# The last 64 tokens' values and gates in fp32, their products in column halves; the first keys on ScalarE's queue, the last rows stored in two parts, and a new order

## The chip, the cores and the metric

The kernel runs on one core of one Trainium2 chip. The metric is the device time of one execution in microseconds, lower is better. A core has a matrix engine (TensorE; PE in the profile, its weight loads PEld), VectorE (DVE), ScalarE (ACT), GpSimd (POOL) and SyncE (SP), which here issues the DMAs. Each engine works through its own instructions in the order in which the program lists them and waits where a semaphore has not been reached. Matmuls write into PSUM, 8 banks of 512 fp32 columns; DVE and ACT empty them.

## What is computed

Two parts, one feeding the other, for 8 batches of 576 tokens.

```python
# part 1: linear attention, 8 heads of 64, 128 features
proj = x @ w_phi                          # x is q or k
proj = proj - max(abs(proj), axis=-1)
phi  = concat([exp(proj), exp(-proj)])
kv   = phi(k).T @ v ;  z = sum(phi(k))
x    = (phi(q) @ kv) / (phi(q) @ z + 1e-6)    # 576 tokens x 512 (all heads side by side)
...
# part 2: 4 experts of head size 64, causal softmax attention, best 2 of 4 by gate
logits = x @ w_gate
for e in range(4):
    q, k, v = x @ wq[e], x @ wk[e], x @ wv[e]
    a  = softmax(causal(q @ k.T / 8))
    ye = a @ v @ wo[e]
    out += (e among the best two) * weight[e] * ye
```

## The kernel before, in words

The work is cut into 32 pairs of heads (four pairs make a batch) for part 1 and 8 batches of two expert groups (g = 0 and 1) for part 2. Each is a set of Python generators that yield one step after the other; a step belongs to one engine. The table `PICKS` holds two letters for each step: which generator goes next, and which PSUM bank it takes or whether ACT or DVE does a copy. So the whole order of every engine is a string that was written ahead, and `in_order` pins it. No rule in the program decides anything at run time; engines only wait for each other's semaphores.

Part 1, for a pair: `load_k`, `load_q`, `load_v` issue loads on SP two pairs ahead; `stream_k` and `stream_tail` project keys (L355, and L403 for the last 64 tokens); `center` (L389, L391) subtracts the row maximum on DVE; ACT takes two exponentials; `stream_kv` forms kv (L403); `stream_q`, `phi_q` project queries (L355), reduce over partitions on POOL (L494) and exponentiate; `stream_n` multiplies (L403); `normed` divides on DVE; `turn_x` transposes on DVE, writes to DRAM (`xd`) and reads it back as x with features on partitions, tile `xl`. x is then split into `xh` (fp32r) and `xl` (the rest), so that a product of full accuracy is three fp32r products: high by high, high by low, low by high.

Part 2, for a batch (`stream_b`): `proj_t` projects q and k of a group (L180), `proj_v` projects values and gate logits of all experts at once: for each of five token blocks j (four of 128 tokens, the last of 64) 12 products of 260 columns, 4 chunks of 128 features by the three fp32r combinations. `evac_v` copies a block from PSUM to `vl`. `scores` forms q @ k.T (L622), `soft` masks and copies, `post` takes the maximum (POOL, L494), subtracts (DVE, L740), exponentiates (ACT) and multiplies with the values (L403), `norm_y` divides and applies the gate weight, `turn_y` transposes (L446), `project_out` multiplies with `wo` (L180), `evac_o` copies to `ot`, `store` writes 128 rows of the output. `gates` works out the gate weights on DVE from the logits in `vl`. In batches 0 to 6 the order of parts is p0 v0 s0 p1 s1 (projections, values, scores); in the last batch it is p0 s0 p1 s1 v0.

The PSUM writes of L180 use the whole array (128 rows by 128 columns); L355 and L622 use it as two halves of 64 rows, L403 as two halves of 64 columns. An fp32 product of the program shows in the trace as two matmul instructions, an fp32r one as one.

At the start `keep_warm` puts 96 small bf16 products (L180, tile `warm`) on PE between the first projections. `split_piece` splits the weights into high and low parts; the values' and gates' weights (`vg`) come in two pieces of 520 columns.

The lines of the values' loop that the change is about:

```python
            for j in range(NJ):
                m = min(128, S - 128 * j)
                kc, ps = yield Step('PE', [k for c in xk for k in c], 'c', has('av', b - 1, 1) if b else has('w', 2))
                ...
                        mm(ps[:m, 0:260], xs[c][x_][:, 128 * j:128 * j + m],
```

## Time and profile before

| | |
|---|---|
| time, median of 3 runs | 567.36 us (566.82 to 567.86) |
| the profiled execution | 567.63 us, of which the span of its records is 565.8 us |
| TensorE clock granted | full in all 40 slices of the span |
| PE busy | 98% of the span |
| DVE, ACT, POOL busy | 86%, 70%, 34% |
| DMA | 62.37 MB, 40.9% of 16 engines' span |

All sums below are made against the profiled execution, which is 0.27 us above the median. A busy share is an average over the whole span; the views by stretch and the chain of waits tell which engine is waited for at a place.

### The profile page before, as it was taken

What the parts mean: (1) busy time and instruction counts of PE and PEld (TensorE: products, weight loads), DVE (VectorE), ACT (ScalarE), POOL (GpSimd) and SP (SyncE); (2) the same over time, 40 slices, a digit from 0 to 9 for tenths busy, and PEclk for the clock granted to TensorE, in tenths of its full rate; (3) what the DMA queues carried; (4) which work ended last, traced back from release to release, by engine and by line L of the source; (5) the groups of instructions that cost most, each with busy time, mean ns of one, the idle gap of its engine ahead of it and who ended that gap; (6) DMA issues with size and microseconds to landing.
All of it is one profiled execution on the core that took longest, in us unless ns stands there. A gap on an engine that the chain in (4) does not pass through costs nothing.

```text
span 565.8 us, 22762 instructions
## 1 busy us (share of the span) xinstructions
PE 555.6 (98%) x9744; PEld 524.6 (93%) x9744; DVE 486.3 (86%) x1246; ACT 395.7 (70%) x748; POOL 193.3 (34%) x78
## 2 busy tenths in 40 slices
PE   8999999999999999999999999999999999999997
PEld 7888899999999999999999999899999999999996
DVE  6899889889799988998998899899688897895893
ACT  4888888857748676686776596496676776665662
POOL 3735552323120752235503222522252430302320
PEclk9999999999999999999999999999999999999999
DMA  6978564533634653243534426334541121321013
GB/s 162 238 194 198 155 161 95 124 91 103 135 100 113 155 131 93 85 134 90 125 99 105 137 56 150 89 106 133 131 123 54 47 61 36 98 83 46 2 44 127
DMA packets 83317, 62.37 MB, mean 110 GB/s; under 512 B 47248, under 2 KB 66064, under 8 KB 83216
## 3 DMA queue, kind: packets, MB, share of 16 engines
q1 hardware_dynamic: 83216, 60.92, 40.9%
q8 instruction: 77, 1.26, 1.0%
q14 instruction: 24, 0.20, 0.1%
HBM read 42.02 MB, written 18.87 MB: 108 GB/s over the span
## 4 chain that ended last, share of the span: by engine, by line
PE 92%; DVE 3%; ACT 2%; issue 1%; ACTq 0%; DVEq 0%
PE ps_c L180 38%; PE ps_c L403 35%; PE ps_c L355 11%; PE ps_c L622 8%; PE ps_c L446 1%; ACT u L189 1%; DVE top L654 0%; DVE st L740 0%; ACT ek L191 0%; DVE gw L723 0%; DVE gs L721 0%; DVE xl L185 0%; DVE u L504 0%; DVE yl L185 0%; ACT mx L191 0%
## 5 line engine op out<-in xcount | busy, mean ns | idle before, releaser
L494 POOL PARTITION_ALL_REDUCE mx<-u x32 | 126.2, 3962 | 157.7 <-ACT u L189 106.8
L180 PE MATMUL ps_c<-xh,qk 128*128 128x320 f32 (+1 forms) x512 | 107.1, 300 | 0.5 <-DVE yl L185 0.5
L191 ACT ACTIVATE ek<-ek 128x1152 f32<-128x1152 f32 x64 | 74.8, 1169 | 20.2 <-DVE ek L391 19.3
L180 PEld LDWEIGHTS ps_c<-xh,qk 128*128 128x128 f32 x512 | 83.3, 189 | 2.3 <-DVE yl L185 0.7
L403 PE MATMUL ps_c<-v_in,ek 128*64 128x65 f32 x2560 | 81.6, 222 | 0.7 <-ACT u L189 0.7
L403 PEld LDWEIGHTS ps_c<-v_in,ek 128*64 128x64 f32 x2560 | 78.0, 137 | 3.9 <-ACT u L189 0.8
L189 ACT COPY st<-ps_c 128x288 f32<-128x288 f32 (+1 forms) x120 | 52.4, 503 | 34.1 <-DVE ps_c L642 29.4
L494 POOL PARTITION_ALL_REDUCE tops<-top x15 | 54.2, 3617 | 63.2 <-DVE top L654 63.2
L180 PE MATMUL ps_c<-xl,qk 128*128 128x256 f32 (+1 forms) x256 | 75.7, 296 | 0.0
L403 PE MATMUL ps_c<-kv,mx 128*64 128x65 f32 x1152 | 62.3, 223 | 1.8 <-ACT kv L189 1.4
L389 DVE TENSOR_REDUCE pmax<-ps_c 128x4 f32<-128x512 f32 (+1 forms) x96 | 51.3, 548 | 13.6 <-PE ps_c L355 7.5
L403 PE MATMUL ps_c<-kv,u 128*64 128x65 f32 x1152 | 59.9, 221 | 0.7 <-issue 0.7
L180 PE MATMUL ps_c<-vg,xh 128*128 128x260 f32 (+1 forms) x320 | 59.0, 285 | 0.0
L740 DVE TENSOR_TENSOR st<-st,tops 128x1152 f32<-128x1152 f32 (+4 forms) x75 | 57.4, 818 | 0.1
L189 ACT COPY u<-ps_c 128x256 f32<-128x256 f32 (+3 forms) x131 | 44.1, 423 | 15.7 <-PE ps_c L355 15.0
L391 DVE TENSOR_TENSOR ek<-ps_c,pmax 128x512 f32<-128x512 f32 (+1 forms) x96 | 52.0, 554 | 3.5 <-PE ps_c L403 1.1
L191 ACT ACTIVATE st<-st 128x1152 f32<-128x1152 f32 (+3 forms) x60 | 49.0, 866 | 8.4 <-DVE st L740 8.0
L403 PEld LDWEIGHTS ps_c<-kv,mx 128*64 128x64 f32 x1152 | 48.4, 138 | 5.1 <-ACT kv L189 2.3
L180 PE MATMUL ps_c<-yh,wo 128*128 128x256 f32 (+1 forms) x256 | 52.1, 298 | 0.0
L403 PEld LDWEIGHTS ps_c<-kv,u 128*64 128x64 f32 x1152 | 48.1, 138 | 0.9 <-issue 0.9
L180 PEld LDWEIGHTS ps_c<-xl,qk 128*128 128x128 f32 x256 | 48.5, 190 | 0.0
L403 PE MATMUL ps_c<-vl,st 128*64 128x65 f32 x1500 | 47.6, 222 | 0.7 <-issue 0.4
(110 smaller groups left out, 1187.2 us busy)
## 6 DMA issues: line engine op xcount, KB each, us to landing
v_in<-in_v_dram SPq DMA_DIRECT2D x32, 320.0 KB, 4.2
q_in<-in_qt_dram SPq DMA_DIRECT2D x64, 144.0 KB, 3.4
xl<-xd SPq DMA_DIRECT2D x32, 288.0 KB, 3.1
out_dram<-ot SPq DMA_DIRECT2D x32, 288.0 KB, 2.1
k_in<-in_kt_dram SPq DMA_DIRECT2D x32, 160.0 KB, 3.7
xd<-xt SPq DMA_DIRECT2D x64, 80.0 KB, 2.0
k_in<-in_kt_dram SPq DMA_DIRECT2D x32, 128.0 KB, 3.6
xd<-xt SPq DMA_DIRECT2D x64, 64.0 KB, 1.8
```

Of the source, the lines that this page charges most:

```text
L180: nc.tensor.matmul(o, a, b, start=start, stop=stop, skip_group_check=True)
L189: nc.scalar.copy(o, i)
L191: nc.scalar.activation(o, i, func, **kw)
L355: nc.tensor.matmul(o, a, b, start=True, stop=True, skip_group_check=True)
L389: dve(n * 128, [mk], [pk]).tensor_reduce(out=m[:, us], in_=src, axis=AX.X, op=ALU.max, apply_absolute_value=True)
L391: dve(n * 128, [(f'ek{p % EKB}1', us.start)], [pk, mk]).tensor_tensor(out=ek2[p % EKB][:, 1, us, :], in0=src, in1=m[:, us].unsqueeze(2).to ...
L403: nc.tensor.matmul(o, a, b, start=start, stop=stop, skip_group_check=True)
L446: nc.tensor.transpose(ps[:, 128 * n:128 * n + k], o[0:k, i, :], ident[0:k, 0:k])
L494: nc.gpsimd.partition_all_reduce(o, i, 128, op)
L622: nc.tensor.matmul(pp_[e][:, o:o + q1 - q0], kk2[k_][r, 128 * j:128 * j + 128], q2[q_][r, q0:q1], start=m == 0, stop=m == 2, skip_group_ch ...
L740: dve(2 * n, [sj[j]], [*key, mk], port=True).tensor_tensor(out=a, in0=a, in1=tops[x][0:m, :, 128 * j:], op=ALU.subtract)
```

## The change

1. The last block of `proj_v` (64 tokens, 12 products of 260 columns) goes. A new generator `tail_v` takes its place: for each of the 4 feature chunks two fp32 products of 130 columns, one into PSUM partitions 0 to 63 (experts 0 and 1 with their logits), one into partitions 64 to 127 (experts 2 and 3), as halves of 64 columns of the array (`column_mm`). It is spawned at the first part of a batch, so that its step can stand anywhere from there. Two copies of 130 columns (ACT or DVE) take the place of one of 260.
2. It needs x and the weights unsplit. The weights are copied by POOL into a new tile `wvf` (`whole_w`, 6 copies at the start). x's last 64 tokens come by an additional DMA for each pair from `xd` into `xf` (32 KB, 128 rows of 256 bytes), issued by SP behind the read of `xl`.
3. The first pair's three key loads are issued by ACT instead of SP.
4. The last 128 output rows are stored in two parts, columns 0 to 255 as soon as they are copied, then 256 to 575.
5. `col`, `row` and `warm` lie in tiles that are used later (`ot`, `ge`); this frees room for the new tiles.
6. `PICKS` is a new string: the order of all engines, the banks, and the choice of ACT or DVE for the copies. Counted over the order of each engine, ACT gets all 6 of DVE's copies to `kv` and all 10 of DVE's copies to `ot`, 12 of the 16 new copies to `vl`, and both casts of `vg`; DVE gets 2 casts of `yh` and 1 of `qk`. The number of warm products stays 96, and so does every other count of PE's instructions.

```diff
--- before.py
+++ after.py
@@ -50,51 +50,51 @@
 
 CODE = "ABCDEFGHIJKLMNOPQRSTUVWXYZabcdefghijklmnopqrstuvwxyz0123456789-_"
 PICKS = (
-    "BAAADADABABABABAAAAAAAAAAAAAAAAAAAGROANAGjNANACAG1OAOAG6PAOAEZPIQIQIPIDAFEBAPIPICANANIDAEAEAAAAAAAE1QIPIPIPIIAHAAAAAAAAA"
...
+    "BAAADACACADAEAAAAAAAAAAAAAAAAAAAHROAOAHjOAOAF1PIQIQIPIAAAAAAH5QAPAHaPAPADADAGECAEAQIQIOAOIJAFAFAF-RIQIQIQIOAOAIAGBPICAPI"
...
 )
 
 
@@ -206,12 +206,14 @@
 
     copies_sb = copies
 
-    def load(o, i, w, r=(), rate=90.0):
-        nc.sync.dma_start(o, i)
-
-    warm = sb("warm", [128, 128], BF16)
+    def load(o, i, w, r=(), rate=90.0, eng='SP'):
+        (nc.scalar if eng == 'ACT' else nc.sync).dma_start(o, i)
+
+    ot = [sb(f"ot{i}", [128, S]) for i in range(2)]
+    ge = sb("ge", [128, 5, 4, 4])
+    warm = ge.rearrange("p a b c -> p (a b c)").bitcast(BF16)[:, 0:128]
     nc.vector.memset(warm, 1.0)
-    col, row = sb("col", [128, 128]), sb("row", [128, 32])
+    col, row = ot[0][:, 0:128], ot[1][:, 0:32]
     nc.vector.memset(col[:, 0:1], 0.0)
     for k in range(7):
         n = 2 ** k
@@ -266,11 +268,11 @@
     nc.vector.memset(vl[:, :, :, 65:66], 1.0)
     nc.vector.memset(vl[64:128, NJ - 1], 0.0)
     lg = vl[:, :, :, 0]
-    ge = sb("ge", [128, 5, 4, 4])
     gt, gs = sb("gt", [128, 3, 5, 4]), sb("gs", [128, 2, 5])
     gw = sb("gw", [128, 5, 4])
     ys = [[sb(f"y{p}{g}", [128, S], F32R) for p in "hl"] for g in range(2)]
-    ot = [sb(f"ot{i}", [128, S]) for i in range(2)]
+    wvf = sb("wvf", [128, WVG])
+    xf = [sb(f"xf{i}", [128, 64]) for i in range(PXB)]
 
     wsp = {}
 
@@ -286,7 +288,7 @@
     def split_piece(name, c0, c1, st, src):
         hi, lo = wsp[name][0:2]
         key, m = st.tensor.name, c1 - c0
-        yield Step('SP', pred=has('w', 1 if name == 'wo' else 0))
+        yield Step('SP', pred=has('wvf', c0 - 520) if name == 'vg' and c0 else has('w', 1 if name == 'wo' else 0))
         load(st[:, 0:m], src[:, c0:c1], key, rate=50.0)
         st_ = Step(copies_sb(m), [key], port=True)
         yield st_
@@ -298,6 +300,7 @@
         else:
             h_, l_ = (t[:, c0:c1].rearrange("p (c n d) -> p c n d", n=4, d=65) for t in (hi, lo))
             x = st[:, 0:m].rearrange("p (c x) -> p c x", x=260)
+            plan.spawn(whole_w(key, x, c0, c1))
             for c in range(2):
                 copy(st_.eng, 256, h_[:, c, :, 1:65], x[:, c, 0:256].rearrange("p (n d) -> p n d", d=64), [hk], [key], 0.52)
             copy(st_.eng, 8, h_[:, :, :, 0], x[:, :, 256:260], [hk], [key], 0.52)
@@ -306,6 +309,14 @@
                 sub_lo(256, l_[:, c, :, 1:65], x[:, c, 0:256].rearrange("p (n d) -> p n d", d=64), h_[:, c, :, 1:65], lk, [key, hk])
             sub_lo(8, l_[:, :, :, 0], x[:, :, 256:260], h_[:, :, :, 0], lk, [key, hk])
 
+    def whole_w(key, x, c0, c1):
+        yield Step('POOL', [key])
+        f_ = wvf[:, c0:c1].rearrange("p (c n d) -> p c n d", n=4, d=65)
+        for c in range(2):
+            nc.gpsimd.tensor_copy(f_[:, c, :, 1:65], x[:, c, 0:256].rearrange("p (n d) -> p n d", d=64))
+        nc.gpsimd.tensor_copy(f_[:, :, :, 0], x[:, :, 256:260])
+        done.add(('wvf', c0))
+
     def load_phi():
         yield Step('SP')
         load(wf, wts[:, 0:WP], 'wphi')
@@ -337,11 +348,11 @@
 
     def load_k():
         for p in range(NPAIRS):
-            yield Step('SP', pred=(lambda: ('main_k', p - IB) in done and ('tail_k', p - IB) in done) if p >= IB else None)
+            yield Step('SP' if p else 'ACT', pred=(lambda: ('main_k', p - IB) in done and ('tail_k', p - IB) in done) if p >= IB else None)
             x, key = k_in[p % IB], f'k_in{p % IB}'
-            load(x[0:64, :], kt[p][:, 0:KC], (key, 0), rate=60.0)
-            load(x[64:128, 0:512], kt[p][:, 768:1280], (key, 1), rate=60.0)
-            load(x[64:128, 512:KC], kt[p][:, 640:768], (key, 2), rate=60.0)
+            load(x[0:64, :], kt[p][:, 0:KC], (key, 0), rate=60.0, eng='SP' if p else 'ACT')
+            load(x[64:128, 0:512], kt[p][:, 768:1280], (key, 1), rate=60.0, eng='SP' if p else 'ACT')
+            load(x[64:128, 512:KC], kt[p][:, 640:768], (key, 2), rate=60.0, eng='SP' if p else 'ACT')
             done.add(('load_k', p))
 
     def load_q():
@@ -541,8 +552,9 @@
         for a, (t0, t1) in enumerate(XROWS):
             load(hbm[:, :, t0:t1], xt[k][32 * a:32 * a + 32, :, 0:t1 - t0], (f'xd{k}', a), [b])
         done.add(('xw', p))
-        yield Step('SP', [(f'xd{k}', a) for a in range(4)], pred=(lambda: p < PXB or ('px', (p - PXB) // NP) in done))
+        yield Step('SP', [(f'xd{k}', a) for a in range(4)], pred=(lambda: p < PXB or all((x, (p - PXB) // NP) in done for x in ('px', 'pt'))))
         load(lo.bitcast(F32), xd[k], [f'xr{i}', f'xl{i}'], [(f'xd{k}', a) for a in range(4)])
+        load(xf[i], xd[k][:, 512:S], f'xf{i}', [(f'xd{k}', a) for a in range(4)], rate=32.0)
         done.add(('xd', p))
         xr = [f'xr{i}']
         st_ = Step(copies_sb(S), xr, port=True)
@@ -660,8 +672,8 @@
 
         def proj_v():
             wvg = wsp["vg"]
-            for j in range(NJ):
-                m = min(128, S - 128 * j)
+            for j in range(4):
+                m = 128
                 kc, ps = yield Step('PE', [k for c in xk for k in c], 'c', has('av', b - 1, 1) if b else has('w', 2))
                 n = 0
                 for c in range(4):
@@ -672,9 +684,26 @@
                         n += 1
                 plan.spawn(evac_v(j, m, kc, ps))
 
+        def tail_v():
+            xk_ = [f'xf{(b * NP + c) % PXB}' for c in range(NP)] + [('vg', 2, c0) for c0 in (0, 520)]
+            kc, ps = yield Step('PE', xk_, 'c', has('av', b - 1, 1) if b else (lambda: ('wvf', 0) in done and ('wvf', 520) in done), tiling=(128, 64))
+            for c in range(NP):
+                for e in range(2):
+                    o = 260 * c + 130 * e
+                    column_mm(ps[64 * e:64 * e + 64, 0:130], xf[(b * NP + c) % PXB], wvf[:, o:o + 130], c == 0, c == 3, kc, [xk_[c], xk_[4 + c // 2]], 130)
+            done.add(('pt', b))
+            for e in range(2):
+                st = Step(copies(130), [kc], hot=True)
+                yield st
+                copy(st.eng, 130, vl[0:64, 4, 2 * e:2 * e + 2, 0:65], ps[64 * e:64 * e + 64, 0:130].rearrange("p (n d) -> p n d", d=65), ['vs4'], [kc])
+            plan.release('c', (kc, ps))
+            done.add(('v', b, 4))
+
         yield Step('PE', (), None, lambda: all_x(*range(b * NP, b * NP + NP))() and all(('w', i) in done for i in (0, 1, 4)))
         for part in ORDER[b == B - 1]:
             yield Step('PE')
+            if part == ORDER[b == B - 1][0]:
+                plan.spawn(tail_v())
             g = int(part[-1])
             if part[0] == 'p':
                 yield from proj_t(0, g)
@@ -820,8 +849,15 @@
 
     def store(b, t):
         oks = [('ot', t % 2, p_[0]) for p_ in PARTS]
-        yield Step('SP', oks, pred=lambda: all(('ot', b, t, p_[0]) in done for p_ in PARTS))
-        load(out[b, 128 * t:128 * t + 128, :], ot[t % 2], ('out', b, t), oks)
+        last = b == B - 1 and t == 3
+        yield Step('SP', oks[:1] if last else oks, pred=(lambda: ('ot', b, t, 0) in done) if last else lambda: all(('ot', b, t, p_[0]) in done for p_ in PARTS))
+        if b < B - 1 or t < 3:
+            load(out[b, 128 * t:128 * t + 128, :], ot[t % 2], ('out', b, t), oks)
+        else:
+            for n, (s0, s1) in enumerate(PARTS):
+                if n:
+                    yield Step('SP', [oks[n]], pred=has('ot', b, t, s0))
+                load(out[b, 128 * t:128 * t + 128, s0:s1], ot[t % 2][:, s0:s1], ('out', b, t, n), [oks[n]])
         done.add(('out', 4 * b + t))
 
     for gen in (load_phi(), keep_warm(), zeros(), load_k(), load_q(), load_v(), stream_k(), stream_tail(), stream_q(), weights(w_qk, ('w', 1)), weights(w_vg, ('w', 2)), weights(w_wo, ('w', 3)), stream_kv(), stream_n(), stream_s()):
```

How the rows move, at three places.

TensorE, batch 0, the end of the values before the change, followed by the first scores (`vg` weights, `xh` and `xl` chunks, numbers are buffers):

```order
L180 MATMUL ps_c3_64<-vg_185,xl3_153 128x260
L180 MATMUL ps_c1_62<-vg_185,xh0_146 64x260 x2
L180 MATMUL ps_c1_62<-vg_185,xl0_147 64x260
L180 MATMUL ps_c1_62<-vg_185,xh1_148 64x260 x2
L180 MATMUL ps_c1_62<-vg_185,xl1_149 64x260
L180 MATMUL ps_c1_62<-vg_185,xh2_150 64x260 x2
L180 MATMUL ps_c1_62<-vg_185,xl2_151 64x260
L180 MATMUL ps_c1_62<-vg_185,xh3_152 64x260 x2
L180 MATMUL ps_c1_62<-vg_185,xl3_153 64x260
L622 MATMUL ps_c5_66<-qh_167,kkh_169 128x288
```

and TensorE, batch 0, with the change, ahead of the first projection of the batch (the key rows are a later pair's):

```order
L366 MATMUL ps_c4_65<-wf_121,k_in0_107 128x128
L414 MATMUL ps_c5_66<-wvf_181,xf0_182 64x130 x2
L414 MATMUL ps_c5_66<-wvf_181,xf1_183 64x130 x2
L414 MATMUL ps_c5_66<-wvf_181,xf2_184 64x130 x2
L414 MATMUL ps_c5_66<-wvf_181,xf3_185 64x130 x2
L414 MATMUL ps_c2_63<-wf_121,k_in0_107 64x128 x2
L180 MATMUL ps_c7_68<-xh0_146,qk_188 128x256
```

The 12 products behind the values are gone, and 8 narrower ones stand ahead of the batch's first projection, next to a key tail that uses the array in the same halves.

VectorE, last batch, around the first scores (L642 masks them; L415 to L440 divide the result of batch 6, group 1), before:

```order
L586 SCALAR_TENSOR_TENSOR ql_168<-ps_c6_67,qh_167 128x320
L642 TENSOR_TENSOR ps_c3_64<-ps_c3_64,mask_95 128x128
L642 TENSOR_TENSOR ps_c2_63<-ps_c2_63,mask_95 128x128
L415 TENSOR_SCALAR sc1_164<-ps_c0_61 128x5
L415 TENSOR_SCALAR sc1_164<-ps_c5_66 128x5
L420 RECIPROCAL ps_c5_66<-sc1_164 128x10
L421 TENSOR_TENSOR sc1_164<-ps_c5_66,gw_177 128x10
L434 TENSOR_TENSOR yq1_166<-ps_c0_61,sc1_164 128x4x64
L440 TENSOR_SCALAR yq1_166<-ps_c0_61,sc1_164 64x64
L434 TENSOR_TENSOR yq1_166<-ps_c5_66,sc1_164 128x4x64
L642 TENSOR_TENSOR ps_c1_62<-ps_c1_62,mask_95 128x128
```

and with the change:

```order
L185 TENSOR_TENSOR kkl_170<-ps_c4_65,kkh_169 128x320
L426 TENSOR_SCALAR sc1_164<-ps_c0_61 128x5
L426 TENSOR_SCALAR sc1_164<-ps_c7_68 128x5
L431 RECIPROCAL ps_c7_68<-sc1_164 128x10
L432 TENSOR_TENSOR sc1_164<-ps_c7_68,gw_176 128x10
L445 TENSOR_TENSOR yq1_166<-ps_c0_61,sc1_164 128x4x64
L451 TENSOR_SCALAR yq1_166<-ps_c0_61,sc1_164 64x64
L445 TENSOR_TENSOR yq1_166<-ps_c7_68,sc1_164 128x4x64
L654 TENSOR_TENSOR ps_c5_66<-ps_c5_66,mask_95 128x128
L654 TENSOR_TENSOR ps_c6_67<-ps_c6_67,mask_95 128x128
```

The seven dividing instructions now stand ahead of the first two masks instead of behind them.

SyncE, the first loads of the program, before:

```order
L210 DMA wf_121<-in_wts_dram 128x128
L210 DMA q_in0_109<-in_qt_dram 64x576 x2
L210 DMA q_in1_110<-in_qt_dram 64x576 x2
L210 DMA k_in0_107<-in_kt_dram 64x640
L210 DMA k_in0_107<-in_kt_dram 64x512
L210 DMA k_in0_107<-in_kt_dram 64x128
L210 DMA k_in1_108<-in_kt_dram 64x640
```

and ScalarE's first rows with the change (SyncE's list there goes on from `q_in0` straight to `k_in1`, then `q_in1`):

```order
L210 DMA k_in0_107<-in_kt_dram 64x640
L210 DMA k_in0_107<-in_kt_dram 64x512
L210 DMA k_in0_107<-in_kt_dram 64x128
L189 ACT_TABLE_LOAD
L189 COPY u0_126<-ps_c1_62 128x2x5x32
```

The first keys no longer stand behind four query loads, and ScalarE issues three loads ahead of its table load.

## Rows read from the trace of the kernel before

**Rows 1.** The page: busy time of PE (part 1), and the chain of work that ended last by engine (part 4).

```profile
PE 555.6 (98%) x9744; PEld 524.6 (93%) x9744; DVE 486.3 (86%) x1246; ACT 395.7 (70%) x748; POOL 193.3 (34%) x78
...
PE 92%; DVE 3%; ACT 2%; issue 1%; ACTq 0%; DVEq 0%
```

**Rows 2.** Busy time by stretch: stretch in us, its length, busy us of PE, PEld, DVE, ACT and POOL with counts, granted PE clock, DMA share, GB/s.

```profile
0.00:20.00 20.00, 18.00 (x256) 15.47 (x258) 14.73 (x62) 11.84 (x20) 9.78 (x9) 1.00 0.73 194
20.00:70.00 50.00, 48.24 (x1174) 42.47 (x1170) 43.85 (x99) 42.70 (x74) 25.85 (x7) 1.00 0.75 189
...
190.00:250.00 60.00, 60.00 (x1003) 56.87 (x1003) 55.23 (x126) 46.12 (x83) 24.52 (x9) 1.00 0.43 113
```

**Rows 3.** Who PE waited for: waiter, releaser, us in total, times, longest. The first and the last of seven rows; the seven add up to 6.1 us.

```profile
PE ps_c L403 <- issue: 1.5, 3, 0.7
...
PE ps_c L403 <- ACT st L191: 0.2, 1, 0.2
```

**Rows 4.** Timeline of PE, batch 0, the last value block (128*64 is the stationary tile) and the first scores: start, duration from first start to last end, instruction, count.

```profile
82.92 0.40 PE L180 MATMUL ps_c<-vg,xh 128*64 128x260 f32 x2
...
84.23 0.28 PE L180 MATMUL ps_c<-vg,xl 128*64 128x260 f32 x1
84.44 0.40 PE L622 MATMUL ps_c<-qh,kkh 64*128 64x288 f32 x2
```

**Rows 5.** Timeline of PE, three places with fp32 products in column halves (tile 128*64), each with the row that follows it.

```profile
62.08 0.44 PE L403 MATMUL ps_c<-wf,k_in 128*64 128x128 f32 x4
62.35 2.50 PE L403 MATMUL ps_c<-v_in,ek 128*64 128x65 f32 x80
64.78 1.24 PE L355 MATMUL ps_c<-q_in,wf 64*128 64x320 f32 x8
...
70.26 0.44 PE L403 MATMUL ps_c<-wf,k_in 128*64 128x128 f32 x4
70.63 0.39 PE L180 MATMUL ps_c<-xh,qk 128*128 128x256 f32 x1
...
546.39 3.14 PE L403 MATMUL ps_c<-vl,st 128*64 128x65 f32 x100
549.35 3.15 PE L403 MATMUL ps_c<-vl,u 128*64 128x65 f32 x100
```

**Rows 6.** Groups of instructions by form: line, engine, operation, tiles, shapes, count, busy us, mean ns of one, idle before. Copies that are moved or resized, on ACT, DVE and POOL.

```profile
L189 ACT COPY ot<-ps_c 128x320 f32<-128x320 f32 x28 | 12.2, 436 | 7.8 <-PE ps_c L180 6.2 <-DMA out_dram<-ot 1.6
L189 ACT COPY kv<-ps_c 128x260 f32<-128x260 f32 x26 | 9.8, 375 | 5.2 <-PE ps_c L403 5.0
L189 ACT COPY ot<-ps_c 128x256 f32<-128x256 f32 x26 | 9.7, 376 | 7.1 <-DMA out_dram<-ot 6.1 <-DVE top L654 0.9
L189 ACT COPY vl<-ps_c 64x260 f32<-64x260 f32 x5 | 1.8, 369 | 2.2 <-PE ps_c L180 2.0
...
L202 DVE COPY kv<-ps_c 128x260 f32<-128x260 f32 x6 | 2.5, 416 | 0.0
...
L635 POOL COPY top<-st 128x256 f32<-128x256 f32 x15 | 6.1, 405 | 115.8 <-ACT st L189 97.9 <-ACT gt L191 14.2 <-DVE sc L421 3.6
```

**Rows 7.** Timelines of the last batch: PE's product with the values of batch 6, DVE's masks and division behind it, the two reductions on POOL, DVE's last subtractions and ACT's last exponential.

```profile
517.17 3.22 PE L403 MATMUL ps_c<-vl,st 128*64 128x65 f32 x100
...
521.02 0.50 DVE L642 TENSOR_TENSOR ps_c<-ps_c,mask 128x128 f32<-128x128 f32 x2 [0.54 <-PE ps_c L622]
521.43 0.22 DVE L415 TENSOR_SCALAR sc<-ps_c 128x5 f32<-128x5 f32 x2
...
523.01 1.00 DVE L642 TENSOR_TENSOR ps_c<-ps_c,mask 128x128 f32<-128x128 f32 x4
...
528.81 3.58 POOL L494 PARTITION_ALL_REDUCE tops<-top  x1 [5.55 <-DVE top L654]
...
541.95 3.58 POOL L494 PARTITION_ALL_REDUCE mx<-mx  x1 [7.91 <-DVE mx L654]
...
545.57 3.76 DVE L740 TENSOR_TENSOR u<-u,mx 128x1152 f32<-128x1152 f32 x5 [0.19 <-POOL mx L494]
...
549.42 1.06 ACT L191 ACTIVATE u<-u 128x1024 f32<-128x1024 f32 x1 [0.20 <-DVE gw L719]
```

**Rows 8.** Timeline of the start, all engines: the six first key loads, ACT's table load and first copies, the first key products, DVE's first work on them, and two reads of x at SP.

```profile
1.00 1.28 ACT L189 ACT_TABLE_LOAD   x1 [1.00 <-DVE ps_c L171]
...
3.68 3.80 SPq L210 DMA_DIRECT2D k_in<-in_kt_dram  x6
...
5.93 2.52 ACT L189 COPY u<-ps_c 128x320 f32<-128x320 f32 x8 [3.65 <-PE ps_c L355]
...
6.95 1.57 PE L355 MATMUL ps_c<-wf,k_in 64*128 64x128 f32 x16
...
8.45 1.29 DVE L389 TENSOR_REDUCE pmax<-ps_c 128x4 f32<-128x512 f32 x2 [2.98 <-ACT u L189]
...
34.08 1.06 SPq L210 DMA_DIRECT2D xl<-xd  x2
```

**Rows 9.** The end: ACT's last copy (timeline), and from the page's part 6 the DMA issues: count, KB each, median us from issue to landing.

```profile
562.05 0.42 ACT L189 COPY ot<-ps_c 128x320 f32<-128x320 f32 x1 [0.79 <-PE ps_c L180]
...
out_dram<-ot SPq DMA_DIRECT2D x32, 288.0 KB, 2.1
...
xd<-xt SPq DMA_DIRECT2D x64, 80.0 KB, 2.0
```

88 lines of the change are left out of this document (44 added, 44 removed).

## Prediction, made before the changed kernel was run

> **What bounds the kernel now.** First the page: PE is busy for 98% of the span, and 92% of the chain that ended last is PE's own work; no other engine has more than 3% [rows 1]. So I ask of each edit what it takes from PE or adds to it, and of each move what it makes PE wait for. A busy share says little about waits, so next the stretches: from 190 to 250 us PE is busy all 60 us, while DVE has 55.23; in the first 20 us PE lacks 2.00 us, from 20 to 70 us 1.76 [rows 2]. Then the list of PE's waits: its seven rows add up to 6.1 us, 1% of the span, and the longest are under a microsecond or lie at the very start [rows 3]. The granted clock is full everywhere [rows 2], so no product is slowed by it. The kernel is therefore bound by the sum of PE's products, and a product that goes is worth its pitch, as long as what stands behind it on PE is ready earlier too.
>
> **The last value block.** Before, its 12 products start at 82.92 us, the twelfth at 84.23: 1.31 us for 11 pitches, 0.119 us each, so 1.43 us a batch [rows 4]. After, 8 fp32 products of 130 columns run in column halves, 16 matmul instructions. No row has 130 columns; two have the same form. 80 instructions of 65 columns take from 62.35 to 64.78, 2.43 us, 0.0304 us each; 100 of them take from 546.39 to 549.35, 0.0296 us each [rows 5]. Twice the columns gives 0.059 to 0.061 us. Four of 128 columns take 0.27 us to the next group, 0.0675 us each, 0.0686 us for 130 [rows 5]. Sixteen cost 0.95 us by the first and 1.10 us by the second. I take 0.97: the long groups have no entry from other work in them. The gain is 1.43 - 0.97 = 0.46 us a batch, 0.33 to 0.48, and over 8 batches **3.7 us (2.6 to 3.9)**.
>
> Entering another split of the array costs: four key tails followed by the same split take 0.27 us, the same four followed by full-array products 0.37 us [rows 5], so 0.10 us a change. The order of PE has 154 such changes before and 153 now, because each of the eight new groups stands beside key tails, products with kv or products with values, which use the same halves. I take nothing. The Trainium skill (TensorEngine Tiling (Array Packing), Key Properties) says that changing the tiling mode drains the engine, which speaks against putting column halves among full-array products; the trace agrees, with those 0.10 us. By that rule alone, with two changes for each new group, the gain would shrink by 16 x 0.10 = 1.6 us; by the order it stays whole.
>
> **Its copies.** One copy of 260 columns on 64 rows (0.369 us on ACT) becomes two of 130, which have no row; each lies between 0.18 us, half of that, and 0.37 us [rows 6]. The choice of engine matters more. Six `kv` copies and ten `ot` copies leave DVE at about 0.416 us each and cost ACT 6 x 0.375, 6 x 0.376 and 4 x 0.436 us, 6.3 us [rows 6]. With the other exchanges ACT gains some 8 us on 395.7 and DVE, the fuller engine at 486.3, loses some 6 us [rows 1]. This costs nothing on the path; if ACT's gaps did not hide a copy, a wait of 0.4 us would appear where PE needs a bank.
>
> **The new inputs.** POOL makes six copies: four of 256 columns at 0.405 us, two small ones for which I take no more than that, 1.6 to 2.4 us [rows 6]. POOL is busy 9.78 + 25.85 of the first 70 us [rows 2], so its idle time hides them; uncovered they would delay one reduction by 2.4 us at most. SP issues 32 more reads, each like an `xl` read, 0.53 us [rows 8], right behind that read and on the same data. They are small, and the products wait for `xl`'s split as well, which comes later. About four fall before the first projection, 2.1 us of SP's time; the three key loads that leave SP give back 3 x 0.63 = 1.9 us [rows 8]. No net cost; the bounds are half a microsecond either way.
>
> **The first keys.** SP issues them from 3.68 us, as the sixth load and later, and the first key products start at 6.95 us [rows 8]. ACT could issue from 1.00 us, where its table load now begins, and after three issues of 0.63 us and 1.28 us of table load be free at 4.2 us, ahead of its first copy at 5.93 [rows 8]. The keys could be some 1.5 us earlier at PE, and DVE, which idles 2.98 us before its first work on them [rows 8], could start as much earlier. Little of it arrives: until the first projection at 70.63 us [rows 5] DVE is busy for 43.85 of 50 us and PE for 48.24 [rows 2], and the 96 warm products stay. I take 0.3 us of gain, between a loss of 0.8 (new waits in the new order) and a gain of 1.5.
>
> **The last batch.** Here the cover gets thinner, and this is where a gain could be lost. Behind the last scores stand values, part of the output projection and two products with values. With 12 products fewer, the last product with values comes 1.43 us sooner after those scores, and it needs ACT's last exponential, which ends at 549.42 + 1.06 = 550.48 us; that product, which starts at 549.35, wants it after 40 of its instructions, at 550.53 [rows 5, 7]. The slack is 0.05 us. In addition the eight new products stand between the product with batch 6's values and the batch's first scores, so those scores are 0.97 us later on PE. Against this stands what DVE does: before, it waited 0.54 us for the scores, masked two of them (0.50 us) and divided batch 6's result only then, 521.43 to 523.01 [rows 7]. Now the division stands first and runs while PE does the new products. From 523.01 on the chain is DVE, POOL (to 532.39), DVE, POOL (541.95 to 545.53), DVE (545.57 to 549.33), ACT, with hardly an idle gap [rows 7]. PE's old product ends at about 520.2; the division, 1.6 us, is then through at about 522.1, the masks at 522.5, where before both were through at 523.0. So the chain moves forward by about 0.5 us, as much as PE's own work does. I charge nothing; without DVE's help 0.97 + 0.46 = 1.4 us would be lost.
>
> **The last store.** 288 KB take 2.1 us from issue to landing, 80 KB 2.0 [rows 9]; the last part is now 160 KB. By these rows it lands 0.1 us sooner, at best 0.4 if size counted more than they show. I take 0.1. ACT makes all last copies; its last one starts 0.79 us after the one before and waits for PE [rows 9], so one of 0.376 us more fits.
>
> **Sum.** 567.6 - 3.7 - 0.3 - 0.1 = 563.5 us against the profiled execution; the median stands 0.27 us lower, so I forecast **563.3 us**. A measurement of this kernel can tell about 0.2%, 1.1 us, from no change.
>
> **Rivals.**
>
> *PE waits for DVE instead (566.2 to 568.4).* PE gets 4 us less work and DVE was at 55.23 of 60 us in a full stretch [rows 2]; the waits of 6.1 us [rows 3] could grow by what was saved: 567.3. For it: every step has a new place, and the slack at the end is 0.05 us. Against it: DVE loses 6 us itself. 10%.
>
> *The last batch's cover is lost.* 563.3 + 1.4 = 564.7 us, if the division on DVE doesn't get done ahead of the scores. 13%.
>
> *The keys' head start comes through.* The chain of the start ends 1.5 us earlier instead of 0.3: 562.1, or 561 with some of the 3.8 us that PE lacks in the first 70 us [rows 2]. 17%.
>
> *The halves do not run side by side at 130 columns: slower.* The place is the new group in each batch. Alone, 130 columns cost half of a 260-column pitch for each pass, 0.06 us, and an instruction of two passes 0.119; sixteen take 1.90 us against 1.43, 0.47 us more in each batch. 567.4 + 3.8 - 0.4 = 570.8 us. It decides where an instruction passes 1.43/16 = 0.089 us. Against it: at 65 columns an instruction takes 0.030 us where one alone would take 0.06, and at 128 columns 0.0675 us, under the point [rows 5]. 3%. The Trainium skill (FP8 and Floating Point Precision, TensorE Precision Notes) gives four passes for true fp32, which without halves would make the new block 8 x 4 x 0.06 = 1.9 us, the same as here; the rows show half of that.
>
> The forecast with small shifts has 52%. The last 5% are new waits of over 5 us, from SP or POOL at the start.
>
> **Range and chances.** The forecast's own bounds are -3.9 - 1.5 - 0.4 and -2.6 + 0.8: 561.6 to 565.6. To hold eight in ten I go to some of PE's present waits on one side and into the first rival on the other: 561.0 to 566.1. Faster by over 0.2% (below 566.2) come the forecast, the second and third rival and a little of the first, 83%; within 0.2% most of the first, 9%; slower 8%.
>
> **What would show it.** Right: 16 instructions of the new form take 0.95 to 1.1 us in each batch; the first scores of the last batch find DVE through with the division; PE's waits sum to 5 to 7 us; the first key products start near 5.5 us. Wrong: a new group over 1.4 us; a wait of PE over 1 us in its last product with values; or PE's waits above 9 us, with DVE or ACT as releasers.

## Result and profile after

The changed kernel takes **570.93 us** (median of 13 runs, 568.28 to 572.63), the kernel before on the same chip 567.86 us (13 runs, 566.60 to 569.38): a ratio of 1.0051 (1.0035 to 1.0067). It is slower by 3.1 us; 563.3 us (561.0 to 566.1) had been forecast. The profiled execution took 572.0 us with a span of 569.9 us.

The page of the kernel after, as [rows 1]: busy time of PE, and the chain that ended last.

```profile
PE 555.2 (97%) x9776; PEld 520.7 (91%) x9776; DVE 487.3 (86%) x1231; ACT 401.5 (70%) x771; POOL 196.3 (34%) x84
...
PE 83%; DVE 7%; ACT 4%; DMA 3%; SPq 1%; issue 1%; POOL 1%; ACTq 0%; DVEq 0%; POOLq 0%
```

PE has as much busy time as before, though it has less to do; its share of the chain fell from 92% to 83%, and DVE, ACT and DMA took what it lost. DVE's busy time did not fall. Busy time by stretch, columns as in [rows 2]:

```profile
0.00:20.00 20.00, 18.37 (x210) 14.93 (x212) 13.47 (x58) 11.02 (x17) 8.35 (x9) 1.00 0.67 176
20.00:70.00 50.00, 44.47 (x1068) 38.24 (x1065) 41.21 (x91) 39.46 (x68) 31.55 (x13) 1.00 0.69 171
...
190.00:250.00 60.00, 60.00 (x1063) 57.45 (x1063) 52.74 (x126) 44.77 (x86) 23.30 (x7) 1.00 0.42 113
```

The loss shows in the second row: from 20 to 70 us PE lacks 5.5 us where it lacked 1.8, and DVE has 2.6 us less work in there. PE's waits, as in [rows 3], the longest and the last of 13:

```profile
PE ps_c L414 <- issue: 1.7, 2, 1.4
PE ps_c L414 <- ACT kv L189: 1.6, 1, 1.6
...
PE ps_c L366 <- DVE ek L402: 0.2, 1, 0.2
```

The 13 add up to 10.9 us where seven added up to 6.1. The longest has no releaser in the profile ("issue"). The list shows only a part of the loss: ahead of the first projection PE executes the same products as before and one new group, and its busy time there grew from 66.8 to 72.0 us, by more than that group's 0.94. The records of those products are hardly longer than before but overlap less, so what is lost between them counts as busy.

Next the timeline of PE: batch 3's new group with its neighbours, and the place of the first projection, as [rows 4, 5].

```profile
284.83 0.46 PE L414 MATMUL ps_c<-vl,st 128*64 128x65 f32 x10
285.12 1.06 PE L414 MATMUL ps_c<-wvf,xf 128*64 128x130 f32 x16
286.01 1.16 PE L414 MATMUL ps_c<-v_in,ek 128*64 128x65 f32 x34
...
78.36 1.11 PE L414 MATMUL ps_c<-wvf,xf 128*64 128x130 f32 x16
79.30 0.39 PE L414 MATMUL ps_c<-wf,k_in 128*64 128x128 f32 x4
79.62 0.39 PE L180 MATMUL ps_c<-xh,qk 128*128 128x256 f32 x1
```

A new group takes 0.89 us (285.12 to 286.01), 0.94 in batch 0. The first projection starts at 79.62 us instead of 70.63 [rows 5]. From there to the end of the span it is 490.3 us; before, 565.8 - 70.6 = 495.2 us. So the work behind the first projection gained 4.9 us, 0.94 of which went in front of it with batch 0's group, so 4.0 us net; and the start lost 79.62 - 70.63 - 0.94 = 8.05 us. These are figures of one execution of each kernel, and the changed kernel's, at 572.0 us, is 1.1 us above its median.

Where in the start? The numerator products, phi(q) @ kv, mark the way; each pair has one. The fifth and the sixth, before, then after:

```profile
49.46 0.45 PE L403 MATMUL ps_c<-kv,mx 128*64 128x65 f32 x8 [0.26 <-ACT kv L189]
...
58.74 0.45 PE L403 MATMUL ps_c<-kv,mx 128*64 128x65 f32 x8 [0.76 <-ACT kv L189]
```

```profile
51.90 0.45 PE L414 MATMUL ps_c<-kv,mx 128*64 128x65 f32 x8
...
65.51 0.45 PE L414 MATMUL ps_c<-kv,mx 128*64 128x65 f32 x8 [1.61 <-ACT kv L189]
```

PE is 2.4 us late at the fifth (and was 2.6 late at the first, 24.41 us against 21.82), 6.8 at the sixth and 8.05 at the seventh (74.00 against 65.95). So 2.4 us are lost in the first 24 us, 4.3 between the fifth and the sixth and 1.3 behind that. Of the 4.3, 1.4 are the wait without a releaser, at 52.5 to 54.0 us, inside the fifth.

The start, as [rows 8] but with the queries and POOL's first reduction, before:

```profile
1.18 2.46 SPq L210 DMA_DIRECT2D q_in<-in_qt_dram  x4
...
7.33 3.94 POOL L494 PARTITION_ALL_REDUCE mx<-u  x1 [6.37 <-ACT u L189]
```

and after:

```profile
0.73 1.93 ACTq L210 DMA_DIRECT2D k_in<-in_kt_dram  x3
1.20 1.18 SPq L210 DMA_DIRECT2D q_in<-in_qt_dram  x2
2.42 1.87 SPq L210 DMA_DIRECT2D k_in<-in_kt_dram  x3
4.34 1.23 SPq L210 DMA_DIRECT2D q_in<-in_qt_dram  x2
6.09 1.43 PE L366 MATMUL ps_c<-q_in,wf 64*128 64x320 f32 x4 [0.30 <-DMA q_in<-in_qt_dram]
7.11 0.42 PE L366 MATMUL ps_c<-wf,k_in 64*128 64x128 f32 x1
8.88 3.94 POOL L505 PARTITION_ALL_REDUCE mx<-u  x1 [8.44 <-ACT u L189]
10.62 1.24 PE L366 MATMUL ps_c<-q_in,wf 64*128 64x320 f32 x8
```

The first keys are issued 3 us sooner and reach PE no sooner: 7.11 us against 6.95. In PE's order they stand behind query products, for whose queries PE now waits (0.30 us), and the second pair's queries are issued at 4.34 us, behind the second pair's keys. The first reduction is 1.55 us late. The store: ACT's last copy, as [rows 9].

```profile
566.64 0.43 ACT L189 COPY ot<-ps_c 128x320 f32<-128x320 f32 x1 [0.22 <-PE ps_c L180]
```

POOL's new copies of the weights, as [rows 6]:

```profile
L316 POOL COPY wvf<-ot 128x256 f32<-128x256 f32 x4 | 2.7, 749 | 0.0
...
L317 POOL COPY wvf<-ot 128x8 f32<-128x8 f32 x2 | 1.8, 886 | 0.0
```

### The profile page after: what moved, and what is told of

It is laid out like the page before. It is cut to its first block, busy times and chain, and to the rows that moved or that the text cites. A ratio compares the mean times of both kernels' runs of the same rounds, so it can differ in the third digit from the quotient of the medians.

```text
span 569.9 us, 22880 instructions
## 1 busy us (share of the span) xinstructions
PE 555.2 (97%) x9776; PEld 520.7 (91%) x9776; DVE 487.3 (86%) x1231; ACT 401.5 (70%) x771; POOL 196.3 (34%) x84
## 4 chain that ended last, share of the span: by engine, by line
PE 83%; DVE 7%; ACT 4%; DMA 3%; SPq 1%; issue 1%; POOL 1%; ACTq 0%; DVEq 0%; POOLq 0%
PE ps_c L180 33%; PE ps_c L414 31%; PE ps_c L366 11%; PE ps_c L634 7%; PE ps_c L457 1%; DMA q_in<-in_qt_dram 1%; SPq L210 1%; DVE top L666 1%; DMA v_in<-in_v_dram 1%; ACT ek L191 1%; ACT u L189 1%; DVE u L769 1%; DVE st L769 1%; POOL mx L505 1%; ACT st L189 1%
## 5 line engine op out<-in xcount | busy, mean ns | idle before, releaser
L769 DVE TENSOR_TENSOR st<-st,tops 128x1152 f32<-128x1152 f32 (+4 forms) x75 | 59.3, 844 | 0.1
L414 PEld LDWEIGHTS ps_c<-vl,st 128*64 128x64 f32 x1500 | 45.4, 138 | 3.3 <-ACT st L191 1.6
```

Source lines behind the costliest of these rows:

```text
L414: nc.tensor.matmul(o, a, b, start=start, stop=stop, skip_group_check=True)
L769: dve(2 * n, [sj[j]], [*key, mk], port=True).tensor_tensor(out=a, in0=a, in1=tops[x][0:m, :, 128 * j:], op=ALU.subtract)
```

## Experiments

Each run was timed in five rounds against the kernel before on its chip (567.3 to 567.9 us there). "First projection" is the start of PE's first product with `qk`: 70.63 us before, 79.62 after. It is read, like every place in a trace, from one execution of each kernel. "Seam" is the place where a run goes over from the old order to the new one.

**e1_tail_old_order.** Kernel before, its order untouched, with the halves.

```diff
+                nc.gpsimd.tensor_copy(f_[:, c, :, 1:65], x[:, c, 0:256].rearrange("p (n d) -> p n d", d=64))
...
+        load(xf[i], xd[k][:, 512:S], f'xf{i}', [(f'xd{k}', a) for a in range(4)], rate=32.0)
...
+                if j == 4:
+                    for c in range(NP):
+                        for e in range(2):
+                            o = 260 * c + 130 * e
+                            column_mm(ps[64 * e:64 * e + 64, 0:130], xf[(b * NP + c) % PXB], wvf[:, o:o + 130], c == 0, c == 3, kc, [], 130)
```

> The kernel before, its order untouched, with only the last value block in fp32 column halves, its two copies, POOL's six copies of the weights and SP's 32 reads of 64 columns; first keys stay on SP, the last store stays whole. Theory A (the halves save 0.5 us a batch and the new order's first 80 us lose it): 567.5 - 8 x 0.5 = 563.5 us, 562.5 to 564.5, first projection at 70 to 72 us. Theory B (POOL's copies and SP's reads delay the start): 567.5 - 4 + 5 to 8 = 568.5 to 571.5 us, first projection at 75 to 79 us.

564.85 us, ratio 0.9955 (0.9942 to 0.9967), first projection at 71.03 us. Theory B falls: with POOL's copies and SP's reads the first projection is 0.4 us later, not 4 to 8. The gain is 2.6 us instead of 4.

**e18_old_order_all_parts.** All parts but the new order and the keys' queue.

> Every part of the change (halves, two copies, POOL's copies, SP's reads, last store in two parts) but the new order and the keys' queue: old order throughout, the last value block where it was. It differs from the first run (564.85 us) by the split last store and by two steps instead of one for the copies. Theory A: 564 to 565 us, the last store 0.1 us or less. Rival (the split store or the copies' steps cost): 565.5 us or more.

564.44 us, ratio 0.9944 (0.9924 to 0.9963), first projection at 70.21 us: the fastest kernel of the study, faster than both the kernel before and the changed one. PE in batch 3, where the group stands behind full-array products and ahead of row halves:

```profile
287.55 0.28 PE L180 MATMUL ps_c<-vg,xl 128*128 128x260 f32 x1
287.76 1.11 PE L414 MATMUL ps_c<-wvf,xf 128*64 128x130 f32 x16
288.80 0.40 PE L634 MATMUL ps_c<-qh,kkh 64*128 64x288 f32 x2
```

The product ahead takes 0.21 us instead of its pitch of 0.12, and the group 1.04 instead of 0.89: 1.13 against 0.89. That the way into and out of the halves costs, 0.24 us here (Theory D, quoted further down with e6), is shown in these rows. Of it, 0.09 us was there before the change too: the last of the 12 products took 0.21 us up to the scores (84.23 to 84.44 [rows 4]). So a block in the old place gains 1.43 + 0.09 - 1.13 = 0.39 us, 3.1 us over eight batches; by its ratio e18 gained 3.2. In the new places the eight groups take 7.46 us together, so they gain 8 x 1.43 - 7.46 = 4.0 us, what was found behind the start.

**e2_keys_old_order, e3_keys_on_sp.** The keys' queue alone, in the old and in the new order.

```diff
-            load(x[0:64, :], kt[p][:, 0:KC], (key, 0), rate=60.0)
...
+            q = nc.sync if p else nc.scalar
+            q.dma_start(x[0:64, :], kt[p][:, 0:KC])
...
```

The other two loads move in the same way; e3 moves all three back from ACT to SP in the changed kernel.

> The kernel before with one edit: the three loads of the first keys go to ACT's queue. Theory A (the order is at fault, not this edit): 566.5 to 568 us. Theory C (three issues and the table load on ACT delay its first copies and with them everything up to the first projection): 569 us or more, first reduction on POOL later than its 7.33 us by over 1 us. My prediction's term said -0.3 us, between -1.5 and +0.8.

> The changed kernel with the first keys' loads back on SP, at the same place in the order. Theory A: within 1 us of the changed kernel, 570 to 572 us. Theory C: the first reduction on POOL comes back from 8.88 to about 7.4 us and the time falls by 1.5 us or more, to 569.5 us or less.

e2: 568.61 us, ratio 1.0021 (1.0004 to 1.0039), first projection at 71.04. Slower, by about 1.2 us, and not by Theory C's way: ACT's copies wait for PE, and PE for queries.

```profile
6.04 2.08 PE L356 MATMUL ps_c<-q_in,wf 64*128 64x320 f32 x13 [0.33 <-DMA q_in<-in_qt_dram]
6.88 2.52 ACT L189 COPY u<-ps_c 128x320 f32<-128x320 f32 x8 [2.87 <-PE ps_c L356]
8.28 3.94 POOL L495 PARTITION_ALL_REDUCE mx<-u  x1 [7.33 <-ACT u L189]
```

The queries were issued as early as before (1.17 us); with the keys' loads under way beside them they land later (in the first 12 us a query load takes 4.0 us from issue to landing, the median, and took 2.9 before), and the first reduction starts at 8.28 us instead of 7.33. e3: 569.52 us, ratio 1.0045 (1.0028 to 1.0063); its first reduction is back at 6.68 us, yet its first projection is at 80.31. In its profile PE idled in the first 10 us (7.15 us busy) and had a granted clock of 0.66 from 10 to 20 us, so its trace tells little of the queue. By the ratios it is 0.3 us faster than the changed kernel, inside both intervals: the queue is not the main loss.

**e8_early_start_old, e7_late_start_old.** The changed kernel with the old order in one half of the start. Its first difference on SP, as an example of the edit:

```diff
 L210 DMA q_in_109<-in_qt_dram 64x576 x2
-L210 DMA k_in_108<-in_kt_dram 64x640
-L210 DMA k_in_108<-in_kt_dram 64x512
-L210 DMA k_in_108<-in_kt_dram 64x128
 L210 DMA q_in_110<-in_qt_dram 64x576 x2
+L210 DMA k_in_108<-in_kt_dram 64x640
+L210 DMA k_in_108<-in_kt_dram 64x512
+L210 DMA k_in_108<-in_kt_dram 64x128
```

> The counterpart: old order until behind the fifth numerator product (49.5 us), new order from there on. Theory A1: only the 2.4 us of the first 50 us come back, first projection at 76.5 to 77.5 us, time 568 to 569.5 us. Theory A2: the jump is gone too, first projection at 72.5 to 74 us, time 564 to 566 us.

> The changed kernel, but from behind the fifth numerator product (51.9 us) until the first projection all engines work in the old order; before that and after it in the new. Theory A1 (the 4.4 us lost between 52 and 66 us come from the order of that stretch itself): first projection at 74.5 to 75.5 us, time 565.5 to 567.5 us. Theory A2 (they follow from the 2.4 us by which everything is late at 52 us): first projection at 78 to 80 us, time 569.5 us or more.

e8: 567.70 us, ratio 1.0008 (0.9996 to 1.0021), first projection at 75.11, 490.4 us from there. Between A1 and A2: with the old order in the first 50 us, 4.5 of the 8.05 us come back at the first projection, and 3.5 stay. Of the 4.5, 2.5 stand ahead of the fifth numerator product (49.44 us instead of 51.90) and 2.0 behind it, and 1.4 of these are the wait without a releaser, which e8's trace does not have. In time the ratios differ by 0.0043, 2.4 us. e7: 576.25 us, ratio 1.016; at its seam PE waits 1.9 us for DVE's centring of keys and its clock falls (0.81 from 50 to 66 us, 0.78 to 90). Its first projection is at 79.97 us. With that clock it tells nothing of A1 or A2.

**e11_early_old_keys_sp.** e8 with the keys on SP.

> The run with the old order until 49.5 us and the new one from there, but with the first keys' loads on SP. Theory K (on ACT's queue they move data beside the first queries' loads and make PE wait for the queries: first reduction 8.3 to 8.4 us against 7.3): first reduction back at 7.1 to 7.4 us, first projection 0.5 to 1.2 us sooner, at 74 to 74.6 us, time 566.5 to 567.2 us. Rival (the keys' queue is of no account): 567.5 to 568 us, first projection at 75.1 us.

566.73 us, ratio 0.9993 (0.9984 to 1.0003), first reduction at 6.95, first projection at 74.42 us: Theory K's figures came out, but for a first reduction that is sooner than it said: the queue costs 0.7 us at the first projection and, by the ratios, 0.9 us of time, though the two intervals overlap a little.

**The late half.** After 50 us two queues differ most. ACT: in the kernel before, pair 5's exponentials stand ahead of the copies of queries 7; after, they stand behind seven of them, while ACT idles 4.15 us (before, then after).

```profile
50.98 2.36 ACT L191 ACTIVATE ek<-ek 128x1152 f32<-128x1152 f32 x2 [1.24 <-DVE ek L391]
53.48 0.75 ACT L189 COPY u<-ps_c 128x320 f32<-128x320 f32 x2
```

```profile
56.70 0.75 ACT L189 COPY u<-ps_c 128x320 f32<-128x320 f32 x2 [4.15 <-PE ps_c L366]
58.02 1.60 ACT L189 COPY u<-ps_c 128x320 f32<-128x320 f32 x5 [0.56 <-PE ps_c L366]
59.51 2.36 ACT L191 ACTIVATE ek<-ek 128x1152 f32<-128x1152 f32 x2
```

SP: before, one weight piece stands ahead of the queries of pairs 9 and 10; after, two do. They share one buffer, and the second waits for the first to be split (before, then after).

```profile
54.95 1.52 SPq L210 DMA_DIRECT2D ot<-in_wts_dram  x1
56.57 2.39 SPq L210 DMA_DIRECT2D q_in<-in_qt_dram  x4
```

```profile
63.55 4.86 SPq L210 DMA_DIRECT2D ot<-in_wts_dram  x2
68.47 2.82 SPq L210 DMA_DIRECT2D q_in<-in_qt_dram  x4
```

**e12_exps_ahead** (on e8), **e14_sp_exps_ahead, e15_sp_queries_ahead, e16_sp_both** (on e11) put these back, one by one and together: on ACT, on SP.

```diff
+L191 ACTIVATE ek_120<-ek_120 128x1152 x2
 L189 COPY u_129<-ps_c_65 128x2x5x32
...
-L191 ACTIVATE ek_120<-ek_120 128x1152 x2
```

```diff
+L210 DMA q_in_110<-in_qt_dram 64x576 x2
+L210 DMA q_in_109<-in_qt_dram 64x576 x2
 L210 DMA ot_77<-in_wts_dram 128x320
 L210 DMA ot_77<-in_wts_dram 128x576
-L210 DMA q_in_110<-in_qt_dram 64x576 x2
-L210 DMA q_in_109<-in_qt_dram 64x576 x2
```

> The run with the old order until 49.5 us and the new one from there, with one thing of the old order put back in the late part: DVE's subtraction of pair 5's last key block goes ahead of the transpose, and ACT's two exponentials of pair 5 (2.36 us) go ahead of the copies of queries 7 and 8, for which ACT idles 2.1 us. Theory E (the late loss of 3.5 us is ACT's queue: the exponentials stand behind copies that wait for PE, and PE's next products with kv and numerators wait for them): first projection 1.4 to 2 us sooner, 73.1 to 73.7 us, time 565.7 to 566.4 us. Rival (PE's and SP's order is the loss: four queries and their loads ahead of the keys): first projection within 0.5 us of 75.1 us, time 567.2 us or more.

> Old order until 49.5 us, new order from there, keys on SP (566.73 us, first projection 74.42 us), and pair 5's two exponentials on ACT ahead of the copies of queries 7 and 8, with DVE's subtraction that they need. Theory E (ACT's queue): sixth numerator product 1.5 to 2 us sooner than 60.28, and most of it kept: first projection at 72.6 to 73.2 us, time 565 to 565.6 us. Theory S (SP's queue: the queries of pair 9 come at 67 us whatever PE does before): first projection at 74.0 to 74.5 us, time 566.3 to 567 us.

> Old order until 49.5 us, new order from there, keys on SP, and on SP the four loads of queries 9 and 10 ahead of the two weight pieces, of which the second waits 3.5 us for the buffer of the first. Theory S: queries' loads at 58 instead of 63.25 us, PE's wait of 0.6 us for them gone, first projection 0.5 to 0.8 us sooner, 73.6 to 73.9 us, time 565.9 to 566.3 us. Theory E alone: first projection within 0.3 us of 74.42 us, or later if the weights are now late for the projections.

> Both edits of the two runs before. If the late loss is ACT's queue first and SP's queue behind it (E and S together): first projection 2 to 2.8 us sooner than 74.42, 71.6 to 72.4 us, time 564 to 564.8 us. If neither: 566 us or more.

| run | time, us | ratio (interval) | first projection, us |
|---|---|---|---|
| e12 | 568.53 | 1.0032 (1.0019 to 1.0045) | 76.68 |
| e14 | 567.25 | 0.9995 (0.9976 to 1.0013) | 75.42 |
| e15 | 567.78 | 0.9997 (0.9983 to 1.0010) | 75.79 |
| e16 | 568.84 | 1.0026 (1.0011 to 1.0042) | 75.92 |

None is faster than its base. PE in e11, then in e14, with the granted clock of a stretch of e14 (columns as in [rows 2]):

```profile
60.28 0.45 PE L414 MATMUL ps_c<-kv,mx 128*64 128x65 f32 x8 [1.61 <-ACT kv L189]
...
66.99 1.88 PE L366 MATMUL ps_c<-q_in,wf 64*128 64x320 f32 x8 [0.60 <-DMA q_in<-in_qt_dram]
```

```profile
58.67 0.45 PE L414 MATMUL ps_c<-kv,mx 128*64 128x65 f32 x8 [1.06 <-ACT kv L189]
...
65.97 0.80 PE L366 MATMUL ps_c<-q_in,wf 64*128 64x320 f32 x2 [1.19 <-DMA q_in<-in_qt_dram]
...
68.50:72.10 3.60, 3.60 (x73) 3.45 (x73) 2.44 (x3) 2.99 (x5) 0.49 (x1) 0.60 0.25 59
```

Theory E gives what it said at the sixth numerator product, 1.61 us. Then PE waits for the queries on SP, 1.56 us in two waits instead of 0.60, and behind them its clock falls to the lower of its two levels for most of 3.6 us: a numerator product takes 3.5 us instead of 2.25. With the queries ahead (e15) that wait is gone, but the weight pieces are issued at 61.45 us instead of 57.82. DVE, in whose queue the sum of the cast weights comes next, idles 5.88 us instead of 4.24:

```profile
64.50 0.49 DVE L185 TENSOR_TENSOR qk<-ot,qk 128x320 fp32r<-128x320 f32 x1 [5.88 <-ACT qk L189]
```

Everything behind it in DVE's queue is late, a transpose too (69.11 us instead of 66.96), for which PE then waits 1.27 us. With both (e16) it waits 3.0 us for an exponential of pair 6. So neither edit by itself takes the late loss away: each is right about its wait, and the next queue brings another. What e14 would take without the loss of clock is open; its four executions that kept it took 565.22 to 566.35 us, e11 566.73 in the median.

**The old order in the whole start.** e4_old_start, e5_old_start_mended, e9_old_start_seam2, e13_old_start_keys_sp and e17_old_start_banks take it until the first projection, the new order from there; they differ in what stands at the seam.

> The changed kernel whole (halves, keys on ACT, split last store, POOL's copies, SP's reads), except that all engines work in the order of the kernel before until its first projection; from there on in the new order. Theory A (the new order of the first 80 us is the loss): the first projection is back at 70.5 to 72 us, the rest takes its 490.3 us, so 561.5 to 563.5 us of span and about 563 to 565 us of time. Theories B and C (inputs or keys): 568 us or more, whatever the order.

> As the run before of this kind (changed kernel whole, old order until the first projection, new order from there), but ACT's two copies of batch 0's last value block now stand ahead of the exponentials of pair 7 and not behind those of pair 9, where they made PE wait 4.8 us and its clock fall to half for 6 us. Theory A (only the order of the start is at fault): first projection at 72 to 73 us, then 490.3 us, span 562.5 to 563.5, time 564 to 565.5 us. Rival (the new order's rest cannot use an earlier start: the wait moves behind the first projection): 567 us or more, with PE waiting over 3 us between 75 and 130 us.

> The changed kernel whole, old order until the first projection, new order from there; ACT's two copies of batch 0's last value block stand ahead of pair 8's exponentials, and the projections of batch 0 take the bank that has been free longest, so that none waits for those copies (3.0 us in the run before of this kind). Theory A (the start's order is the loss): first projection at 72.5 to 74 us, the second batch's 16 us later, 490.3 us from the first to the end, time 564.5 to 566 us. Rival (the new order's rest needs the new start): the wait shows up elsewhere before the second batch and the time stays at 568 us or more.

> The changed kernel with the old order until the first projection and the new order from there, first keys' loads on SP; the last value block of batch 0 stands ahead of pair 8's keys in a bank that no projection takes next, and its copies ahead of pair 7's exponentials, so that the seam has no wait. Theory A (the start's order and the keys' queue are the whole loss): first projection at 72 to 73 us, span 562.3 to 563.5, time 563.5 to 565 us. Rival (the new order's rest cannot take up the old start): a wait of over 3 us between 75 and 135 us, 567 us or more.

> Old order until the first projection, new order from there, first keys on SP, and the projections, values and scores of batch 0 in the banks that they had in the kernel before. Theory A (the start's order and the keys' queue are the whole loss): first projection at 72.0 to 72.6 us, the second batch's 16 to 16.4 us later, 474.3 us from there to the end, span 562.4 to 563.2, time 564.2 to 565 us. Rival (the new order's rest costs a wait with any other start than its own): second batch's projections at 90 us or later, 567 us or more.

| run | time, us | ratio (interval) | first projection, us | longest waits of PE behind it, us |
|---|---|---|---|---|
| e4 | 575.03 | 1.0132 (1.0114 to 1.0150) | 72.79 | 4.8 for ACT's copies of the new group |
| e5 | 570.87 | 1.0093 (1.0060 to 1.0126) | 73.69 | 3.0 for the same |
| e9 | 576.62 | 1.0166 (1.0146 to 1.0185) | 75.09 | 6.0 for ACT's exponentials |
| e13 | 569.26 | 1.0025 (1.0009 to 1.0041) | 72.17 | 2.1 for DVE's centring |
| e17 | 582.70 | 1.0246 (1.0218 to 1.0274) | 73.08 | 3.5 for ACT, 3.1 for DVE |

All five bring the first projection back to 72.2 to 75.1 us, three with every part of the change in place (e4, e5, e9) and two with only the keys back on SP, so its order is what made it late. All five miss the time: behind the seam PE waits for copies, exponentials or centring that the new order has in another place. That the changed kernel with an old start takes the forecast time is **not shown**; the nearest, e13, has one long wait left behind the seam, in an execution that kept its clock and took 566.89 us. Eight of the other eleven had a mean clock of 0.996 or 0.997 and took 568.77 to 570.99:

```profile
79.20 0.41 PE L180 MATMUL ps_c<-xh,qk 128*128 128x320 f32 x1 [2.15 <-DVE ek L402]
```

**e6_old_order_tail_moved, e10_old_order_tail_beside.** The old order with the new groups moved next to other products in halves.

> The whole order of the kernel before, first keys on SP, last store in two parts, and the column-half groups moved from behind the full-array value products to a place right behind a product with values (batch 0: behind a key tail), which uses the same halves. Theory D (each entry into and exit from the halves costs PE about 0.1 us; the old place pays two of them in each batch, the new place none): 8 x 0.2 = 1.6 us below the first run's 564.85, 563.3 us, 562.5 to 564. Rival (the place makes no difference, the halves save 0.3 us a batch wherever they stand): 564.5 to 565.2 us.

> Old order, first keys on SP, last store in two parts; the column-half group stands, in batches 1 to 6, right behind the last PE group ahead of the value products that uses halves (keys' tail, kv, numerator or values), its two copies right ahead of the first value copy. Theory D (an entry into the halves and an exit cost 0.09 us and up to 0.1 us; here only the group's own 0.79 us and at most one of them is left): 564.85 - 6 x 0.2 = 563.6 us, 563.0 to 564.3. Rival (each such move opens a new wait, as in the run that moved all eight and lost 10 us to waits of 1 to 3 us): 565.5 us or more.

577.90 us (1.0189) and 596.31 us (1.0515). The moved groups themselves got shorter (0.89 to 0.99 us instead of 1.04, where no wait follows), but a group in a new place holds a bank until its copies run. In e10 PE waits 14.7 us in all for DVE's copies to `vl`, for instance

```profile
296.52 0.80 PE L180 MATMUL ps_c<-vg,xh 128*128 128x260 f32 x2 [4.53 <-DVE vl L202]
```

## Why the prediction was wrong

**The last value block: right.** 0.97 us a batch was taken; 0.89 to 0.99 was measured, by what stands beside it, 4.0 us of gain where 3.7 was forecast; in the old place (e18) it is 1.13 with the way in. The halves run side by side, and that rival is out. The Trainium skill (TensorEngine Tiling (Array Packing), Key Properties) says that a change of the tiling mode drains the engine; the runs agree, with 0.24 us for the way in and out (e18). The forecast held here because the new order puts seven of the eight groups right behind other column halves and five right ahead of some.

**Copies, last batch, last store: right in sum, with one wrong premise.** Behind the first projection the gain is 4.0 us where the terms gave 3.8. PE's one wait in its last product with values is 0.4 us, so the rival on the last batch's cover is out; so is the rival on DVE behind the start, where PE waits for it once, 1.0 us. But DVE did not lose the 6 us that were held against that rival: it is busy 487.3 us, 486.3 before. The moved copies went, and the 32 subtractions that form `xl` took 0.892 us each instead of 0.751 (0.767 in e18, with the old order), 4.5 us in all; why is open. The split store is not shown by itself: e18 and e1 differ by 0.4 us, less than their intervals.

**The new inputs: right in effect, not in size.** POOL's six copies took 4.5 us where 1.6 to 2.4 was taken, and 3.7 in e18. Nothing shows that they cost time: the first projection is 0.4 us late with them in e1, and 0.4 early in e18.

**The first keys: wrong, and with it the sum.** The term was -0.3 us with a loss of at most 0.8 for "new waits in the new order". The start lost 8.05 us at the first projection, and PE's waits of 10.9 us are past the 9 that the prediction had named as its sign of being wrong. By the runs, one execution each, step by step: 0.6 from 70.63 + 0.94 to e13 (inputs, seam and scatter), 2.25 from e13 to e11 (the order after 50 us), 0.7 from e11 to e8 (the keys' queue), 4.5 from e8 to the changed kernel (the order of the first 50 us). In time, the changed kernel is 2.9 us above the kernel before by the ratios, and e18, with the old order and the keys on SP, 3.2 us below it. Two errors stand behind the term. The smaller, 0.7 us by e11 and about 1.2 by e2: the head start was worked out from when ACT can *issue*; what counted was when the *queries* land, and they land later with the keys on the way beside them (e2). The first key products, named for 5.5 us, came at 7.11. The larger: the bound of 0.8 had no row behind it; the order of the start was counted (which engine copies what) and not read queue by queue, though the second pair's keys ahead of its queries, and the queries of pairs 9 and 10 behind two weight pieces, stood in it (what either costs by itself is not shown). The case nearest to what came, new waits of over 5 us from SP or POOL at the start, had been given 5%. The place was right; the releasers were not only these. From 20 us to the first projection PE's waits add up to 5.8 us: 3.0 for ACT, 1.6 without a releaser, 1.0 for loads, 0.2 for DVE.

**Still open:** which step of the order costs most, what the wait of 1.4 us in the fifth numerator product is, and whether any order has both the old start and the new rest.

## What to carry to other kernels

Where a change brings a new order, go through the first stretch queue by queue: for each engine, what stands ahead of the step that another engine waits for, and what that step itself waits for. An early transfer was no gain here, because something that was needed sooner was on its way at the same time (e2). And an order that is written ahead is one piece: none of the six kernels in which single steps were moved (e6, e10, e12, e14 to e16) became measurably faster than its base, while the change of the arithmetic alone, in the old order, kept 3 us.
